# Preparing w_in's low parts: GpSimd adds up the high word's rest, and TensorE gathers three bfloat16 products

## The chip, the cores and the metric

The kernel runs on one core of a Trainium2 chip. The metric is the device time of one execution in microseconds. Several runs were timed; their median is quoted with the lowest and the highest.

## The reference

Eight sequences of 576 tokens go through block attention (8 heads of 64, blocks of 64 tokens that attend only within themselves) and then through a gated MLP with spatial gating. q and k come in scaled up, and the weights arrive as float64.

```python
scores = scale * np.matmul(q_c, k_c.transpose(0, 1, 2, 4, 3))
attn = np.exp(scores - np.max(scores, axis=-1, keepdims=True))
attn = attn / (np.sum(attn, axis=-1, keepdims=True) + 1e-09)
x = np.matmul(attn, v_c)              # then heads side by side: (8, 576, 512)

h = gelu_tanh(x @ w_in)               # w_in: 512 x 1024
u, v = h[..., :512], h[..., 512:]
v_n = (v - mean(v)) / np.sqrt(var(v) + 1e-06) * g_ln
v_s = np.einsum('ts,bsd->btd', w_sg, v_n) + b_sg[None, :, None]
out = x + (u * v_s) @ w_out           # w_out: 512 x 512
```

## The kernel before

**Precision.** Each operand of the MLP's products is kept as two fp32r numbers, a high part `hi` and a low part `lo`, and a product is the sum of three: lo x hi, hi x lo, hi x hi. The large weights come as float64, that is as two 32-bit words, and have to be turned into `hi` and `lo` on the chip. For w_in that is the work of `pair_begin` and `pair_end`, done eight times on pieces of 128 x 512 numbers: four pieces of the v half (one for each 128 rows, steps `W` and `w` of the start-up list) and four of the u half (one for each 128 columns, steps `X` and `x`).

**One piece.** It lands in a staging tile `st` of four words a number (the buffers that later hold w_sg or w_out's parts). `pair_begin` lets ScalarE (ACT) and VectorE (DVE) make three things from the two words: `f`, the high word's value as a float32; `p`, the power of two that belongs to it; and `q`, a bfloat16 that holds the upper bits of the low word on the scale of `p`. `pair_end` has ACT write `hi = -f`, rounded to fp32r. Then TensorE adds up in PSUM what is left: the identity in float32 times `f`, 2^-20 times `q`, -2^-20 times `p` (both in bfloat16, by the tiles `low`), and the identity in fp32r times `hi`. ACT negates the sum into `lo`. All weights of w_in carry a minus sign, which the activation behind the product takes off. In the v half, `v_w_end` then issues the load of a piece of the u half into the same staging tile.

**Order.** Steps of the first two sequences stand in a hand-written list, `START`: `L`, `W`, `w` load, begin and end a v piece, `X` and `x` begin and end a u piece, `S`, `T`, `O` (and `P`, `Q` for two tiles at a time) are scores, transposes and outputs of attention on tiles of 128 tokens, `G` and `g` load and split w_sg, `Y` prepares w_out, `A` loads q, k and v ahead, `D` keeps the TensorE clock up with spare products, and `vBM`, `uBM`, `sBM`, `oBM` are the four kinds of matmul units of the MLP for sequence B. In that phase attention, weight preparation and the first units are woven into each other on all engines. From sequence 2 on a loop runs v, u, s and o units with attention steps in fixed slots. The scheduler keeps each engine's instructions in an order of its own that follows the list, and each engine works through its order strictly one after another.

**Buffers.** The pool `ps_m` has three PSUM buffers `pm` of two banks each, handed out in turn to the scores of the first tiles, to the pieces' sums, and to the units. A unit's buffer comes free when ACT (`v`, `u`) or DVE (`s`, `o`) has read it.

**GpSimd (POOL)** does little: the low parts `xl` of two early tiles, the reciprocal root of the variance in `v_unit` (L461, a [128, 1] operation), and from the third sequence on the last multiplication of the softmax.

Lines that recur below: L130 to L133 `high_word`; L162 and L166 the rest of `pair_begin`; L174 `hi`; L178 the four products; L179 `lo`; L314 scores and L398 outputs of early tiles; L452 `v_unit`'s products, L455 its activation, L460, L461 and L467 to L470 its normalisation; L489 `u_unit`'s products; L509 `s_unit`'s.

Of the kernel before, what the change touches and what calls it, by code (L numbers as in the profile page):

```python
# [10 lines left out]
F32 = mybir.dt.float32  # L11
# [4 lines left out]
BF16 = mybir.dt.bfloat16  # L16
AF = mybir.ActivationFunctionType
ALU = mybir.AluOpType
# [4 lines left out]
P = 128  # L23
DM = 512
DF = 1024
DH = DF // 2
# [17 lines left out]

START = """
L0 A0 L1 A1 L2 L3 A4 W0 S0 W1 D8 w0 S1 W2 T0 w1 S2 O0 T1 W3 w2 S3 O1 T2 M0 w3 S4 O2 T3 v00 X0 O3 G0 T4 v01 x0 X1 O4 A8
v02 x1 X2 v03 X3 v04 u00 x2 g0 g1 u01 x3 g2 P5 g3 u02 g4 T5 u03 T6 s00 P7 Q5 s01 s02 T7 T8 s03 v10 Q7 v11 Y0 v12 Y1
v13 Y2 u10 Y3 u11 Y4 u12 Y5 Y6 u13 Y7 A10 s10 A12 s11 P9 s12 s13 T9 o00 T10 P11 o01 o02 o03 Q9 A14 T11 o10 T12 o11 Q11
S13 A15 o12 T13 o13
"""  # L50
# [30 lines left out]
def block_attention_gated_mlp(ctx: ExitStack, tc: tile.TileContext, qkv, w_in, w_out, w_sg, g_ln, b_sg, out):  # L81
    nc = tc.nc
# [7 lines left out]
    ps_m = ctx.enter_context(tc.tile_pool(name="ps_m", bufs=3, space=PSUM))  # L90
# [11 lines left out]
    ident_r = const.tile([P, P], F32R, name="ident")  # L102
    nc.scalar.copy(ident_r, eye)
    ident = ident_r.bitcast(F32)

    low = [const.tile([P, P], BF16, name=f"low_{i}") for i in range(2)]
    for a, c in zip(low, (2.0**-20, -(2.0**-20))):
        nc.scalar.mul(a, eye, c)
    win_h = const.tile([P, KT, DF], F32R, name="win_h")
    win_l = const.tile([P, KT, DF], F32R, name="win_l")  # L110
# [43 lines left out]
    def pair_begin(n, st):  # L154

        pair = st[:, : 2 * n].rearrange("p (n w) -> p n w", w=2)
        f, p = st[:, 2 * n : 3 * n], st[:, 3 * n : 4 * n]  # L160
        high_word(f, pair[:, :, 1])
        nc.vector.tensor_scalar(p, f, -0x800000, None, op0=ALU.bitwise_and)  # L162

        words = st[:, : 2 * n].bitcast(U16)
        q, lw, top = words[:, :n], words[:, 1::4], p.bitcast(U16)[:, 1::2]
        nc.vector.scalar_tensor_tensor(q, lw, 9, top, op0=ALU.logical_shift_right, op1=ALU.bitwise_or)  # L166

    def pair_end(n, hi, lo, st):

        f = st[:, 2 * n : 3 * n].bitcast(F32)  # L170
        p, q = st[:, 3 * n : 4 * n].bitcast(BF16)[:, 1::2], st[:, : 2 * n].bitcast(BF16)[:, :n]
        ps = ps_m.tile([P, 2, 512], F32, name="pm")[:, 0, :n]
        shape = lambda a: a.rearrange("p (k c) -> p k c", k=hi.shape[1]) if len(hi.shape) == 3 else a
        nc.scalar.mul(hi, shape(f), -1.0)  # L174
        terms = [(ident, f), (low[0], q), (low[1], p), (ident_r, hi)]
        for i, (a, c) in enumerate(terms):
            out_ps = shape(ps) if c is hi else ps
            nc.tensor.matmul(out_ps, a, c, start=(i == 0), stop=(i == len(terms) - 1))  # L178
        nc.scalar.mul(lo, shape(ps), -1.0)  # L179


    def w_out_tile(i, dt=F32R):
# [5 lines left out]
    staged = {}  # L188
# [3 lines left out]
        pair_begin(DH, staged["v", kt])  # L192

    def v_w_end(kt):
        pair_end(DH, win_h[:, kt, DH:], win_l[:, kt, DH:], staged["v", kt])
        u_w_load(kt)

    def v_w_load(kt):
# [3 lines left out]
    def u_w_load(dt):  # L202

        st = staged["u", dt] = w_sg_tile(dt, I32) if dt < 2 else w_out_tile(dt - 2, I32)
        dst = st[:, : 2 * DH].rearrange("p (k c) -> p k c", k=KT)
        nc.sync.dma_start(out=dst, in_=w_in[:, :, 2 * dt * P : 2 * (dt + 1) * P])

    def u_w_begin(dt):
        pair_begin(DH, staged["u", dt])

    def u_w_end(dt):
        cols = slice(dt * P, (dt + 1) * P)
        pair_end(DH, win_h[:, :, cols], win_l[:, :, cols], staged["u", dt])

    def o_w(et, half):
        nonlocal wout_h, wout_l
# [41 lines left out]
    def load_misc():  # L258
        nc.sync.dma_start(out=g_bc, in_=g_ln.broadcast_to([P, DH]))
# [44 lines left out]
    def att_scores(*tiles):  # L304

        scs = []
        for i, t in enumerate(tiles):
            qt = state[t]
            if t < PE_TILES:
                sc = ps_m.tile([P, 2, H, D], F32, name="pm")[:, 0]  # L310
                for h in range(H):
                    for c in range(2):
                        r = slice(c * D, (c + 1) * D)
                        nc.tensor.matmul(sc[r, h, :], qt[r, 0, h, :], qt[r, 1, h, :], start=True, stop=True)  # L314
            else:


                sc = banks[:, :, i * HP * D : (i + 1) * HP * D].rearrange("p c (hp s) -> p c hp s", hp=HP)
                for h in range(H):
                    for c in range(2):  # L320
                        r, o = slice(c * D, (c + 1) * D), slice((h + c) % 2 * D, ((h + c) % 2 + 1) * D)
                        nc.tensor.matmul(sc[o, c, h // 2, :], qt[r, 0, h, :], qt[r, 1, h, :], start=True, stop=True)  # L322
            scs.append(sc)
        for t, sc in zip(tiles, scs):
            softmax_begin(t, sc)
        for t in tiles:
            softmax_end(t)
# [57 lines left out]
    def att_out(*tiles):  # L385

        xos = []
        pm = ps_m.tile([P, 2, 512], F32, name="pm") if tiles[0] >= PE_TILES else None
        for i, t in enumerate(tiles):
            qt, ptT = state.pop(t)  # L390
            if t < PE_TILES:
                vt = qt[:, 2, :, :].rearrange("p (c hp) d -> p c hp d", c=2)
                xo = next_bank()
                for hp in range(HP):
                    for c in range(2):
                        for j in range(2):
                            r = slice(j * D, (j + 1) * D)
                            nc.tensor.matmul(  # L398
                                xo[r, hp, c * D : (c + 1) * D], vt[r, c, hp, :], ptT[r, hp, c * D : (c + 1) * D],
                                start=True, stop=True,  # L400
                            )
                xo = xo.rearrange("p hp (c s) -> p c hp s", c=2)
            else:

                xo = pm[:, :, i * HP * D : (i + 1) * HP * D].rearrange("p c (hp s) -> p c hp s", hp=HP)
                for h in range(H):
                    for c in range(2):
                        j, place = (h + c) % 2, c * HP + h // 2
                        r, o = slice(j * D, (j + 1) * D), slice(h % 2 * D, (h % 2 + 1) * D)
                        nc.tensor.matmul(  # L410
                            xo[o, c, h // 2, :], qt[r, 2, place, :], ptT[r, place].rearrange("p a s -> p (a s)"),
                            start=True, stop=True,
                        )
            xos.append(xo)
        for t, xo in zip(tiles, xos):
            keep(t, xo)
# [138 lines left out]
    def att_slots(b, n):  # L555
# [8 lines left out]
        return slots  # L564

    steps = {
        "L": v_w_load, "M": lambda k: load_misc(), "W": v_w_begin, "w": v_w_end, "X": u_w_begin, "x": u_w_end, "A": ahead,
        "S": att_scores, "T": att_transpose, "O": att_out, "P": lambda t: att_scores(t, t + 1), "Q": lambda t: att_out(t, t + 1),
    }
    for name, f in zip("vuso", (v_unit, u_unit, s_unit, o_unit)):  # L570
# [66 lines left out]
```

## Time and profile before

| | before |
|---|---|
| median of 3 runs | 507.87 us (507.09 to 510.36) |
| span of the profiled execution, first to last instruction | 505.7 us |
| PE busy | 493.4 us |
| DVE busy | 339.2 us |
| ACT busy | 274.2 us |
| POOL busy | 70.0 us |
| mean granted TensorE clock | 0.999 |

For the profiled execution the page gives its span; the runs' times stand beside it and take in launch and end. PE is TensorE's matmuls and PEld its weight loads. A row of the timeline has the start in microseconds from the span's start, the duration, the engine, the line, the operation, the output and inputs by the program's names, the shapes, and in brackets how long the engine had been idle and what ended that. "x2" joins two instructions of the same kind: the duration then runs from the first one's start to the last one's end. A matmul's duration includes the time in which its result drains, so that successive matmuls overlap in these rows. A row of the line view has the busy time and the mean of one in nanoseconds, or the shortest, the median and the longest.

### The profile page before, as it was taken

The numbers are of one execution on the slowest core, as the hardware profiler recorded it, in microseconds if no ns is written. First come the engines' busy times: TensorE is split into PE (matmuls) and PEld (weight loads), VectorE is DVE, ScalarE is ACT, GpSimd is POOL, SyncE is SP. The second block draws the span as 40 slices with busy tenths as digits, with TensorE's granted clock in tenths as the row PEclk, the third lists the DMA queues.
The fourth block names the chain that finished last, engine by engine and source line by source line (L and its number), as shares of the span: only waits on it lengthen the run. The fifth ranks groups of instructions, "written<-read, shape, count | busy, mean of one in ns | idle before, by whom it ended". The sixth has DMA issues, their size and how long they took to land.

```text
span 505.7 us, 12377 instructions
## 1 busy us (share of the span) xinstructions
PE 493.4 (98%) x5238; PEld 457.1 (90%) x5244; DVE 339.2 (67%) x707; ACT 274.2 (54%) x509; POOL 70.0 (14%) x72
## 2 busy tenths in 40 slices
PE   5999999999999999999999999999999999999996
PEld 4667899799998899989999899989999899999996
DVE  7998779987856947585563966676565776536141
ACT  5898667843346674355552774355643766334210
POOL 0112100210201401022100311022100131002000
PEclk9999999999999999999999999999999999999999
DMA  8958010237166113341324204160415200010002
GB/s 336 331 144 224 3 43 2 85 97 197 48 201 199 55 36 93 101 119 46 82 73 148 64 1 128 47 174 2 126 37 160 87 1 3 23 73 0 1 1 93
DMA packets 49595, 46.58 MB, mean 92 GB/s; under 512 B 35202, under 2 KB 39554, under 8 KB 49540
## 3 DMA queue, kind: packets, MB, share of 16 engines
q1 hardware_dynamic: 49540, 45.80, 29.9%
q8 instruction: 41, 0.67, 0.6%
q14 instruction: 14, 0.11, 0.1%
HBM read 36.34 MB, written 9.44 MB: 91 GB/s over the span
## 4 chain that ended last, share of the span: by engine, by line
PE 83%; DVE 7%; ACT 5%; DMA 3%; POOL 1%; issue 1%; DVEq 0%; SPq 0%; ACTq 0%; POOLq 0%
PE pm L509 20%; PE pm L532 19%; PE pm L489 18%; PE pm L452 17%; PE banks L322 3%; PE pm L410 3%; DMA qkv_t<-qkv 2%; PE pm L178 2%; DMA st<-w_out 1%; ACT pt L344 1%; PE pm L314 1%; POOL sm L461 1%; DVE v L470 1%; DVE gl L97 1%; PE pm L577 1%
## 5 line engine op out<-in xcount | busy, mean ns | idle before, releaser
L509 PE MATMUL pm<-wsg,v 128*128 128x288 f32 x768 | 107.9, 296 | 0.0
L509 PEld LDWEIGHTS pm<-wsg,v 128*128 128x128 f32 x768 | 103.9, 189 | 0.3
L532 PE MATMUL pm<-gh,wout 128*128 128x288 f32 x512 | 92.3, 297 | 0.0
L532 PEld LDWEIGHTS pm<-gh,wout 128*128 128x128 f32 x512 | 76.1, 189 | 0.5
L461 POOL TENSOR_TENSOR sm<-sm,neg_half 128x1 f32<-128x1 f32 x36 | 36.6, 1017 | 164.9 <-DVE sm L460 161.5
L358 POOL TENSOR_TENSOR pt<-pt,den 128x512 f32<-128x512 f32 x27 | 29.7, 1113 | 202.2 <-DVE den L357 128.3
L94 ACT CAST gh<-gt 128x576 fp32r<-128x576 f32 x32 | 21.5, 673 | 63.5 <-DVE gt L513 63.5
L532 PE MATMUL pm<-gl,wout 128*128 128x288 f32 x256 | 55.4, 296 | 0.0
L489 PE MATMUL pm<-xh,win_l 128*128 128x288 f32 x256 | 55.4, 298 | 0.0
L489 PE MATMUL pm<-xh,win_h 128*128 128x288 f32 x256 | 55.0, 296 | 0.0
L489 PE MATMUL pm<-xl,win_h 128*128 128x288 f32 x256 | 55.0, 296 | 0.0
L452 PE MATMUL pm<-win_h,xl 128*128 128x512 f32 x128 | 51.6, 403 | 2.0 <-DVE sm L460 0.9
L452 PE MATMUL pm<-win_l,xh 128*128 128x512 f32 x128 | 50.8, 397 | 0.0
L452 PE MATMUL pm<-win_h,xh 128*128 128x512 f32 x128 | 50.7, 396 | 0.0
L513 DVE TENSOR_TENSOR gt<-pm,u 128x576 f32<-128x576 f32 x32 | 24.1, 754 | 39.2 <-PE pm L509 39.1
L540 DVE TENSOR_TENSOR ot<-pm,xf 128x576 f32<-128x576 f32 (+1 forms) x33 | 24.1, 732 | 29.9 <-PE pm L532 29.8
L489 PEld LDWEIGHTS pm<-xh,win_l 128*128 128x128 f32 x256 | 41.5, 188 | 1.0
L532 PEld LDWEIGHTS pm<-gl,wout 128*128 128x128 f32 x256 | 41.5, 189 | 0.0
L489 PEld LDWEIGHTS pm<-xh,win_h 128*128 128x128 f32 x256 | 41.0, 188 | 0.0
L489 PEld LDWEIGHTS pm<-xl,win_h 128*128 128x128 f32 x256 | 41.0, 189 | 0.0
L97 DVE TENSOR_TENSOR xl<-pm,xh 128x512 fp32r<-128x512 f32 (+1 forms) x34 | 21.8, 640 | 26.4 <-ACT xh L94 26.4
L458 DVE BATCH_NORM_STATS2 sm<-hs 128x6 f32<-128x512 f32 x36 | 24.8, 688 | 19.8 <-ACT hs L455 19.6
(121 smaller groups left out, 816.7 us busy)
## 6 DMA issues: line engine op xcount, KB each, us to landing
qkv_t<-qkv SPq DMA_DIRECT2D x32, 512.0 KB, 4.5
out_dram<-ot SPq DMA_DIRECT2D x31, 288.0 KB, 2.1
qkv_t<-qkv SPq DMA_DIRECT2D x124, 64.0 KB, 3.6
qkv_t<-qkv SPq DMA_DIRECT2D x3, 768.0 KB, 11.9
wsg<-w_in SPq DMA_DIRECT2D x4, 512.0 KB, 6.4
wout<-w_in SPq DMA_DIRECT2D x4, 512.0 KB, 6.0
st<-w_out SPq DMA_DIRECT2D x8, 256.0 KB, 3.1
stage<-w_sg SPq DMA_DIRECT2D x5, 288.0 KB, 3.7
```

What stands on the lines that cost most here:

```text
L94: nc.scalar.copy(hi, src)
L97: lo_eng.tensor_tensor(lo, src, hi.bitcast(F32), op=ALU.subtract)
L322: nc.tensor.matmul(sc[o, c, h // 2, :], qt[r, 0, h, :], qt[r, 1, h, :], start=True, stop=True)
L358: (nc.gpsimd if t > last[1] else pick(f"n{t}")).tensor_tensor(pt, pt, den.unsqueeze(2).broadcast_to([P, H, D]), op=ALU.mult)
L452: nc.tensor.matmul(pv, a[:, kt, tok], c[:, kt, DH:], start=(i == 0), stop=(i == 11))
L458: nc.vector.bn_stats(st, h)
L461: nc.gpsimd.tensor_tensor(rs, rs, neg_half, op=ALU.pow)
L489: nc.tensor.matmul(pm[:, j, :HS], a[:, kt, dc], c[:, kt, j * HS : (j + 1) * HS], start=(i == 0), stop=(i == 11))
L509: nc.tensor.matmul(pm[:, j, :HS], a[:, dc], c[:, m, j * HS : (j + 1) * HS], start=(i == 0), stop=(i == len(ops) - 1))
L513: nc.vector.tensor_tensor(gt.rearrange("p (a c) -> p a c", a=2), pm[:, :, :HS], u2[0][:, dt, :].rearrange("p (a c) -> p a c", a=2), op=ALU ...
L532: nc.tensor.matmul(pm[:, j, :HS], a[:, kt, ec], c[:, kt, j * HS : (j + 1) * HS], start=(i == 0), stop=(i == len(ops) - 1),)
L540: nc.vector.tensor_tensor(ot[:, js], pm[:, js, :HS], res[:, js], op=ALU.add)
```

## The change

`pair_end` is cut in two. `pair_high` has ACT write `hi = -f` as before and then GpSimd compute `d = f + hi`, the part of `f` that `hi` does not hold, as a bfloat16, into the staging tile's second quarter of 16-bit words. The new `pair_end` adds up three bfloat16 products: `low[0]` times `q`, `low[1]` times `p`, and a bfloat16 identity times `d`. That identity, `ident_b`, is the upper half of each float32 of the old one. The float32 product with `f` and the fp32r product with `hi` go. For the v half both run in the step `w`, one behind the other. For the u half `x` now runs `pair_high` alone, and a new step `e` runs `pair_end`; in the list the `e` steps stand one or more units behind their `x`.

```diff
-v02 x1 X2 v03 X3 v04 u00 x2 g0 g1 u01 x3 g2 P5 g3 u02 g4 T5 u03 ...
+v02 e0 x1 X2 v03 e1 X3 v04 x2 u00 e2 x3 g0 g1 u01 e3 g2 P5 g3 u02 g4 T5 u03 ...
...
+    ident_b = ident_r.bitcast(BF16)[:, 1::2]
...
-    def pair_end(n, hi, lo, st):
-        f = st[:, 2 * n : 3 * n].bitcast(F32)
-        p, q = st[:, 3 * n : 4 * n].bitcast(BF16)[:, 1::2], st[:, : 2 * n].bitcast(BF16)[:, :n]
-        ps = ps_m.tile([P, 2, 512], F32, name="pm")[:, 0, :n]
+    def pair_parts(n, st):
+        words = st[:, : 2 * n].bitcast(BF16)
+        return words[:, :n], st[:, 3 * n : 4 * n].bitcast(BF16)[:, 1::2], words[:, n : 2 * n]
+
+    def pair_high(n, hi, st):
+        f, d = st[:, 2 * n : 3 * n].bitcast(F32), pair_parts(n, st)[2]
         shape = lambda a: a.rearrange("p (k c) -> p k c", k=hi.shape[1]) if len(hi.shape) == 3 else a
         nc.scalar.mul(hi, shape(f), -1.0)
-        terms = [(ident, f), (low[0], q), (low[1], p), (ident_r, hi)]
-        for i, (a, c) in enumerate(terms):
-            out_ps = shape(ps) if c is hi else ps
-            nc.tensor.matmul(out_ps, a, c, start=(i == 0), stop=(i == len(terms) - 1))
-        nc.scalar.mul(lo, shape(ps), -1.0)
+        nc.gpsimd.tensor_tensor(shape(d), shape(f), hi.bitcast(F32), op=ALU.add)
+
+    def pair_end(n, lo, st):
+        ps = ps_m.tile([P, 2, 512], F32, name="pm")[:, 0, :n]
+        for i, (a, c) in enumerate(zip((*low, ident_b), pair_parts(n, st))):
+            nc.tensor.matmul(ps, a, c, start=(i == 0), stop=(i == 2))
+        nc.scalar.mul(lo, ps.rearrange("p (k c) -> p k c", k=lo.shape[1]) if len(lo.shape) == 3 else ps, -1.0)
...
     def v_w_end(kt):
-        pair_end(DH, win_h[:, kt, DH:], win_l[:, kt, DH:], staged["v", kt])
+        pair_high(DH, win_h[:, kt, DH:], staged["v", kt])
+        pair_end(DH, win_l[:, kt, DH:], staged["v", kt])
         u_w_load(kt)
...
+    def u_w_high(dt):
+        pair_high(DH, win_h[:, :, dt * P : (dt + 1) * P], staged["u", dt])
     def u_w_end(dt):
-        cols = slice(dt * P, (dt + 1) * P)
-        pair_end(DH, win_h[:, :, cols], win_l[:, :, cols], staged["u", dt])
+        pair_end(DH, win_l[:, :, dt * P : (dt + 1) * P], staged["u", dt])
...
-        "X": u_w_begin, "x": u_w_end, ...
+        "X": u_w_begin, "x": u_w_high, "e": u_w_end, ...
```

More of the change, by code (lines that the diff above doesn't have):

```diff
@@ L46 @@
 L0 A0 L1 A1 L2 L3 A4 W0 S0 W1 D8 w0 S1 W2 T0 w1 S2 O0 T1 W3 w2 S3 O1 T2 M0 w3 S4 O2 T3 v00 X0 O3 G0 T4 v01 x0 X1 O4 A8
-v02 x1 X2 v03 X3 v04 u00 x2 g0 g1 u01 x3 g2 P5 g3 u02 g4 T5 u03 T6 s00 P7 Q5 s01 s02 T7 T8 s03 v10 Q7 v11 Y0 v12 Y1
+v02 e0 x1 X2 v03 e1 X3 v04 x2 u00 e2 x3 g0 g1 u01 e3 g2 P5 g3 u02 g4 T5 u03 T6 s00 P7 Q5 s01 s02 T7 T8 s03 v10 Q7 v11 Y0 v12 Y1
 v13 Y2 u10 Y3 u11 Y4 u12 Y5 Y6 u13 Y7 A10 s10 A12 s11 P9 s12 s13 T9 o00 T10 P11 o01 o02 o03 Q9 A14 T11 o10 T12 o11 Q11
@@ L566, in block_attention_gated_mlp @@
     steps = {
-        "L": v_w_load, "M": lambda k: load_misc(), "W": v_w_begin, "w": v_w_end, "X": u_w_begin, "x": u_w_end, "A": ahead,
+        "L": v_w_load, "M": lambda k: load_misc(), "W": v_w_begin, "w": v_w_end, "X": u_w_begin, "x": u_w_high, "e": u_w_end, "A": ahead,
         "S": att_scores, "T": att_transpose, "O": att_out, "P": lambda t: att_scores(t, t + 1), "Q": lambda t: att_out(t, t + 1),
```

## The prediction

> **What bounds the kernel now.** First the page's head, to see which engine could set the time:
>
> ```profile
> span 505.7 us, 12377 instructions
> PE 493.4 (98%) x5238; PEld 457.1 (90%) x5244; DVE 339.2 (67%) x707; ACT 274.2 (54%) x509; POOL 70.0 (14%) x72
> ```
>
> TensorE (PE) is busy in all but 12.3 us, GpSimd (POOL) in 70. That reads as "less PE work is less time". But the change touches only the preparation of w_in, all of it in the first 60 us, so I ask next what that stretch waits for. Here is the busy time of each engine in two stretches, cut where the chain of waits (below) returns to PE and where it leaves it again:
>
> ```profile
> core 0: us, PE busy (x) PEld busy (x) DVE busy (x) ACT busy (x) POOL busy (x), PEclk, DMA share, GB/s
> 10.00:37.70 27.70, 26.07 (x322) 17.76 (x324) 25.89 (x55) 25.10 (x78) 3.54 (x3) 1.00 0.76 254
> 37.70:70.70 33.00, 32.94 (x281) 27.92 (x287) 26.71 (x60) 25.81 (x46) 5.67 (x5) 1.00 0.34 89
> ```
>
> In 10 to 37.7 us three engines are nearly full: PE 26.1, VectorE (DVE) 25.9, ScalarE (ACT) 25.1 of 27.7 us. In 37.7 to 70.7 PE has 0.06 us to spare and DVE 6.3. The clock was 1.00 in both, so no duration here is stretched by it. Now the chain that ended last:
>
> ```profile
> 17.33 0.59 ACT xf L428
> ...
> 20.85 2.38 ACT pt L344 x16
> ...
> 25.03 1.10 DVE den L356
> ...
> 27.62 2.48 ACT pt L344 x16
> ...
> 37.07 0.65 DVE xl L97
> 37.76 1.43 PE pm L452 x5
> ...
> 66.92 3.73 PE pm L509 x28
> 70.67 0.77 DVE gt L513
> ```
>
> It is on PE up to 17.3 us (`xf` there waits for a PE product), alternates between ACT and DVE until DVE's `xl` frees `v02` at 37.76, is PE without a break to 70.67, and goes on from there through what that product starts. So a PE saving counts fully only between 37.76 and 70.67; before that, DVE and ACT have to be done with the same list of work as now. What starts at 70.67 hangs on PE's product, so I let a shift at that point pass to the end unchanged.
>
> **The change, part by part.** *PE's saving.* One pair's slot, x1's, from before:
>
> ```profile
> 42.48 1.02 PE L178 MATMUL pm<-wsg,ident 128*128 128x512 f32 x2
> 43.33 0.38 PE L178 MATMUL pm<-wsg,low 128*128 128x512 bf16 x1
> 43.58 0.59 PE L178 MATMUL pm<-win_h,ident 128*128 128x512 f32 x1
> 44.01 0.39 PE L452 MATMUL pm<-win_h,xl 128*128 128x512 f32 x1
> 44.24 0.40 PE L452 MATMUL pm<-win_l,xh 128*128 128x512 f32 x1
> 14.40 0.60 PE L178 MATMUL pm<-wsg,low 128*128 128x512 bf16 x2
> ```
>
> The float32 product is two instructions. PE is free for the next pair-unrelated product at 44.01, so the pair holds it for 44.01 - 42.48 = 1.53 us. The last row (two bfloat16 products in 0.60, one being 0.38) gives 0.22 us for each bfloat16 product; successive fp32r ones stand 44.24 - 44.01 = 0.23 apart. After: 3 x 0.22 = 0.66, a saving of 0.87 us a pair, 7.0 us for eight. The new stationary operand `ident_b` is every second bfloat16 of a float32 tile, and no row shows such a weight load. The nearest rows:
>
> ```profile
> L178 PEld LDWEIGHTS <-low x16: 97/98/98, 10.8 to 58.4; 128*128 128x128 bf16 x16
> L178 PEld LDWEIGHTS pm<-wsg,ident x8: 187/190/192, 10.2 to 42.5; 128*128 128x128 f32 x8
> ```
>
> Either, 0.10 or 0.19, fits beneath the 0.22 of the product running before it, so I take nothing (at most 0.1 x 8 = 0.8 if it were exposed).
>
> Where do the eight lie? Before, x1, x2 and x3 lie behind 37.76 (3 x 1.53 = 4.59). After, the list places x0's products (e0) behind `v02` too, so four lie there: 4 x 0.66 = 2.64. PE's stretch from 37.76 to 70.67 shrinks by **1.95 us**. That x0's 1.53 us vanish ahead of 37.76 brings nothing of itself: `v02` waits there for DVE's `xl`, not for PE.
>
> *ACT and VectorE.* Their instructions stay: same negation into `hi`, same eviction into `lo`, same bit operations. Nothing gets shorter on the two engines that carry the chain from 17.3 to 37.7.
>
> *GpSimd's eight sums.* `d = f + hi`, 128x512 float32 with two full inputs. The nearest row is GpSimd's `xl` subtraction; beside it what DVE did meanwhile, and the same DVE operations undisturbed:
>
> ```profile
> 18.65 1.28 POOL L97 TENSOR_TENSOR xl<-xf,xh 128x512 fp32r<-128x512 f32 x1 [17.35 <-ACT xh L94]
> 19.18 1.30 DVE L133 SCALAR_TENSOR_TENSOR wout<-wout 128x512 int32<-128x512 int32 x1
> 15.37 0.68 DVE L133 SCALAR_TENSOR_TENSOR wout<-wout 128x512 int32<-128x512 int32 x1
> 24.82 1.27 POOL L97 TENSOR_TENSOR xl<-xf,xh 128x512 fp32r<-128x512 f32 x1 [4.89 <-ACT xh L94]
> 25.03 1.09 DVE L356 TENSOR_SCALAR den<-den 128x8 f32<-128x8 f32 x1
> 30.21 0.17 DVE L356 TENSOR_SCALAR den<-den 128x8 f32<-128x8 f32 x1
> L358 POOL TENSOR_TENSOR pt<-pt,den 128x512 f32<-128x512 f32 x27 | 29.7, 1113 | 202.2 <-DVE den L357 128.3
> ```
>
> A sum should take 1.28 us (between 1.11, the mean with a broadcast input, and, if the bfloat16 output costs more, 2.2, the longest two-input operation GpSimd has here, shown below). More telling is the DVE column: beside GpSimd the L133 took 1.30 instead of 0.68, and an L356 of 0.17 took 1.09 and ended at 26.12, just after GpSimd at 26.09. DVE was held until GpSimd was done: 0.62 and 0.92 us lost, mean 0.77. The first started 0.53 us into GpSimd's 1.28: until then DVE ran a reduction out of PSUM, which was not held.
>
> The Trainium skill ("SBUF — State Buffer", section "SBUF: two separate sides") gives the reason: the two engines share a port pair under "an exclusive lock, not a bandwidth split", taken by GpSimd or by a DVE operation with two SBUF inputs or in a two-port mode, whichever is first, for its whole length. The trace agrees (1.09 against 0.17). By that rule alone a sum that meets only such operations would cost DVE its full 1.28, 10.2 us for eight; the rows above, where part of each sum ran beside a PSUM reader, are what I use.
>
> Most of DVE's list around the sums is of the held kinds (L131 to L133, L162, L166, L356, L358). Ahead of 37.76 lie five sums (w0 to w3, x0): 5 x 0.77 = **3.85 us** of DVE. What can swallow it: DVE's idle time in 10 to 37.7, which is 27.7 - 25.89 = 1.81, of which these waits for others are genuine slack:
>
> ```profile
> 13.16 0.69 DVE L333 TENSOR_REDUCE nmax<-pm 128x8 f32<-128x512 f32 x1 [0.28 <-PE pm L314]
> 23.26 0.17 DVE L356 TENSOR_SCALAR den<-den 128x8 f32<-128x8 f32 x1 [0.27 <-ACT pt L344]
> 32.52 0.70 DVE L458 BATCH_NORM_STATS2 sm<-hs 128x6 f32<-128x512 f32 x1 [0.62 <-ACT hs L455]
> 17.33 0.58 ACT L428 COPY xf<-banks 128x512 f32<-128x512 f32 x1 [0.61 <-PE banks L398]
> ```
>
> 0.28 + 0.27 + 0.62 = 1.17, and from the last row 0.3 of the 0.61 us in which ACT waits for PE, since w0 and w1 are 0.87 shorter each but the next ACT step, w2's `hi`, hangs on DVE. Carried to 37.76: 3.85 - 1.17 - 0.3 = **+2.4 us** (bounds: 0 if the sums meet PSUM readers and idle time, 5 x 1.28 - 0.3 = 6.1 if they meet nothing else). After 37.76 DVE has 6.3 us of slack and three sums cost it 2.3: I take nothing.
>
> *The new wait.* PE's third product waits for ACT `hi`, then GpSimd's 1.28; before, the last product waited for `hi` alone, with 1.3 us of other products ahead of it. Behind it on PE's queue stand scores and transposes. The latest `hi` of the v pairs is w3's:
>
> ```profile
> 24.58 0.69 ACT L174 ACTIVATE win_h<-wout 128x512 fp32r<-128x512 f32 x1
> 55.57 0.75 DVE L256 TENSOR_TENSOR wsg<-bt,bh 1x576 fp32r<-1x576 f32 x1
> ```
>
> It ends at 25.27, GpSimd's `xl` above at 26.09, so `d` is there at about 27.4. `v00` reads the fourth low part in its last three products of twelve, and `v01` waits for DVE anyway, so I take nothing (0 to 1). w3's buffer is released about 2 us later, so on SP's queue the u load behind it, and the qkv and w_sg loads behind that, start as much later; the page gives that load 6.0 us to land, from about 28, and ACT begins x3 some 9 us after that start: hidden. The splits of w_sg must wait for e0 and e1, which read the buffers they go to, some 4 us; DVE's last instruction for them, the second row, ended at 56.3, and `s00` needs them 10 us later: hidden.
>
> **Sum:** -1.95 + 2.4 = about **+0.4 us** on the profiled 505.7, so 506.1. The median of the runs shown, 507.87, is 2.2 above that span (launch and end); predicted 508.3, no change. A measurement of this kernel can tell about 1%, 5.1 us, from none.
>
> **The rivals.** (1) *The holding does not reach PE*: the sums fall into stretches where DVE reads PSUM or waits, and the order of each engine adapts. Then the PE saving stands alone: 505.7 - 1.95 = 503.8 on the span, and with up to 1.2 us of DVE's early waits gone 502.6; plus 2.2, and in the middle of the two, **505.4**. For it: POOL's idle time gives much freedom; against: both rows with GpSimd beside DVE in this stretch show a loss.
>
> (2) *GpSimd's queue becomes the wait* (the slower side). v_unit's reciprocal root (L461) is on the same in-order queue:
>
> ```profile
> 33.70 0.99 POOL L461 TENSOR_TENSOR sm<-sm,neg_half 128x1 f32<-128x1 f32 x1 [7.61 <-DVE sm L460]
> 45.69 2.19 POOL L461 TENSOR_TENSOR sm<-sm,neg_half 128x1 f32<-128x1 f32 x1 [0.97 <-DVE sm L460]
> 47.92 0.72 ACT L469 ACTIVATE v<-hs,sm 128x512 fp32r<-128x512 f32 x1 [1.06 <-POOL sm L461]
> 48.55 0.58 ACT L455 ACTIVATE hs<-pm 128x512 f32<-128x512 f32 x1
> 32.85 0.64 ACT L174 ACTIVATE win_h<-wsg 128x512 fp32r<-128x512 f32 x1
> 49.60 0.43 PE L489 MATMUL pm<-xh,win_l 128*128 128x288 f32 x2
> ```
>
> x0's `hi` (32.85 + 0.64) is ready just before the root at 33.70, and x3's comes about when the one at 45.69 starts. If a sum stands ahead of the root, L469 comes 1.28 later, and behind it in ACT's order the eviction of `v03` (L455, 48.55 to 49.13). The three PSUM buffers then decide: with e1 and e2 at their new places, `u00` (PE, 49.60) takes the buffer that `v03` gives back, a margin of 0.47 us. Two such delays, at x0 and x3, cost 2 x 1.28 = 2.6 on top of my sum: **510.9**. It decides as soon as a sum runs within 0.5 us ahead of a root.
>
> (3) *All of the saving counts*, since early PE time draws the DVE and ACT work forward: -7.0 gives **500.9**. Against it: they have only 1.8 and 2.6 us idle in 27.7.
>
> (4) *It doesn't do what it says*: sums of 2.2 us, as in the second row above, hold DVE 2.19 - 1.28 = 0.9 longer, five times ahead of 37.76: 508.3 + 4.5 = **512.8**.
>
> **How the numbers follow.** Forecast (506.5 to 510) 0.45; rival 1, 0.25; rival 2, 0.18; rival 3, 0.05; rival 4, 0.07. Leaving out rivals 3 and 4 and a little of the edges, the range is 503.9 to 512.0. Faster by over 1% is below 502.8: rival 3 and a tail of rival 1, 0.08. Slower by over 1% is above 512.9: half of rival 4 and the tail of rival 2, 0.09. Within: 0.83.
>
> **What would show it.** In the changed profile: L178-like rows with three bfloat16 products at 0.38 each and no float32 ones; eight new GpSimd rows of about 1.3 us; DVE's busy time up by 4 to 6 us with an unchanged count, in L131 to L166 and L356 rows that read 1.0 to 1.3; `v02` starting near 40 instead of 37.76; PE idle in 10 to 40 us up by some 6 us; `s00` starting within 1 us of 66.75. I am wrong if DVE's rows stay at their old lengths, if `v02` starts before 37 or after 42, or if ACT's waits for L461 grow by over 2 us.

## The result, and the profile after

The changed kernel takes **511.72 us** in the median (511.11 to 512.65, 4 runs), against 507.89 us for the kernel before on the same chip: ratio 1.0075, 95% interval 1.005 to 1.01. It is 3.8 us slower. That lies within the bound of 1% and, by 0.3 us, within the predicted range (up to 512.0), but 3.4 us above the predicted 508.3 and nearer to rival 2 (510.9). The profiled execution has a span of 510.0 us, 4.3 more than before. In the experiments below, three plainly disturbed executions (686, 1667 and 2680 us) are part of the medians but not of the ratios.

Lines have moved: the products are L185 now, `hi` L177, the sum L179, `lo` L186, `v_unit`'s products L462, its root L471, the activation behind the root L479, softmax L368. From the page of the changed kernel, the head:

```profile
span 510.0 us, 12371 instructions
PE 490.7 (96%) x5228; PEld 456.9 (90%) x5228; DVE 342.2 (67%) x707; ACT 274.3 (54%) x509; POOL 82.4 (16%) x80
```

TensorE has 2.7 us less to do and the span is 4.3 us longer. So the time is in waits. VectorE has the same 707 instructions and 3.0 us more. The same stretches as in the prediction, cut where `v02` and the product behind `s00` now stand (us, busy time of each engine with its instructions, granted clock, DMA share, GB/s):

```profile
10.00:41.40 31.40, 23.84 (x316) 17.65 (x315) 28.47 (x56) 24.38 (x76) 10.79 (x9) 0.89 0.68 228
41.40:75.25 33.85, 32.59 (x276) 27.77 (x280) 27.20 (x57) 26.60 (x47) 10.14 (x8) 0.95 0.32 83
```

`v02` starts at 41.40 instead of 37.76, 3.64 later. Up to there DVE has 28.47 us of work instead of 25.89, with one instruction more. From there to the end of `s00`'s first products it is 33.85 us instead of 32.9. And the clock is no longer 1.00 in either stretch. What DVE waited for, ahead of `v02`:

```profile
DVE nmax L343 <- PE pm L324: 2.0, 2, 1.7
```

Before, that wait was 0.28. So the 3.64 consist of 2.58 us of longer DVE work and 1.06 of longer DVE idle time, the latter because scores come late from PE (1.7 more) while DVE's wait for `hs` (0.62) is gone. The rest is best seen at two places of the timeline, both in this fence, with a line of dots between them:

```profile
18.28 1.26 POOL L97 TENSOR_TENSOR xl<-xf,xh 128x512 fp32r<-128x512 f32 x1 [3.40 <-ACT xh L94]
18.40 1.69 DVE L167 SCALAR_TENSOR_TENSOR wout<-wout 128x512 uint16<-128x512 uint16 x1
20.14 0.93 PE L185 MATMUL pm<-wout,low 128*128 128x512 bf16 x2 [2.83 <-DVE wout L167]
...
39.33 0.15 DVE L470 TENSOR_SCALAR sm<-sm 128x1 f32<-128x1 f32 x1
39.44 1.83 POOL L179 TENSOR_TENSOR wsg<-wsg,win_h 128x512 bf16<-128x512 f32 x1 [3.96 <-ACT wout L131]
40.67 0.67 DVE L97 TENSOR_TENSOR xl<-banks,xh 128x512 fp32r<-128x512 f32 x1
41.23 0.55 POOL L471 TENSOR_TENSOR sm<-sm,neg_half 128x1 f32<-128x1 f32 x1
41.40 0.50 PE L462 MATMUL pm<-win_h,xl 128*128 128x512 f32 x1 [2.13 <-DVE xl L97]
41.81 0.72 ACT L479 ACTIVATE v<-hs,sm 128x512 fp32r<-128x512 f32 x1 [1.92 <-POOL sm L471]
43.61 0.65 PE L376 MATMUL banks<-ident,pt 128*128 128x128 f32 x4 [1.26 <-ACT xf L442]
```

At 18.40 GpSimd's `xl`, an old instruction, holds DVE's making of `q`, which takes 1.69 instead of 0.69. PE, whose first product of that piece reads `q`, stands for 2.83 us. Before, the float32 product of `f` stood first in the piece and did not need `q`; the change removed it, and with it PE's cover. The second place is the lower part: x1's sum takes GpSimd until 41.27, the root behind it on the queue had its input from DVE since 39.48, ACT's L479 stands 1.92 us for that root, and then PE 1.26 for ACT's `xf` behind it. Now the clock around those places, PE alone, in steps of 3.4 us cut where the clock changes:

```profile
core 0: us, PE busy (x), PEclk, DMA share, GB/s
16.88:20.30 3.42, 0.59 (x17) 1.00 0.95 311
20.30:23.71 3.41, 3.02 (x17) 0.50 0.03 8
23.71:27.12 3.41, 3.41 (x59) 0.50 0.72 238
40.78:44.19 3.41, 1.53 (x8) 1.00 0.85 260
44.20:47.60 3.40, 3.40 (x37) 0.50 0.86 265
```

Behind the first stall PE is nearly full and runs at half speed for 6.8 us, behind the second for 3.4 us. That makes three candidates: the holding of DVE by the sums, the queue of GpSimd, and PE's stalls with the clock that falls behind them.

### The profile page after: what moved, and what is told of

The parts are those of the page before. It is cut to its first block, busy times and chain, and to the rows that moved or that the text cites. A ratio compares the mean times of both kernels' runs of the same rounds, so it can differ in the third digit from the quotient of the medians.

```text
span 510.0 us, 12371 instructions
## 1 busy us (share of the span) xinstructions
PE 490.7 (96%) x5228; PEld 456.9 (90%) x5228; DVE 342.2 (67%) x707; ACT 274.3 (54%) x509; POOL 82.4 (16%) x80
## 4 chain that ended last, share of the span: by engine, by line
PE 87%; DVE 8%; ACT 2%; issue 1%; DMA 1%; POOL 0%; DVEq 0%; SPq 0%; ACTq 0%
PE pm L519 21%; PE pm L499 20%; PE pm L542 19%; PE pm L462 18%; PE banks L332 3%; PE pm L420 3%; PE pm L324 1%; DMA qkv_t<-qkv 1%; PE pm L185 1%; DVE nmax L343 1%; PE banks L408 1%; DVE gl L97 1%; DVE gt L523 1%; DVE pt L368 1%; DVE blocks L382 1%
## 5 line engine op out<-in xcount | busy, mean ns | idle before, releaser
L368 POOL TENSOR_TENSOR pt<-pt,den 128x512 f32<-128x512 f32 x27 | 29.7, 1113 | 202.0 <-DVE den L367 128.0
L471 POOL TENSOR_TENSOR sm<-sm,neg_half 128x1 f32<-128x1 f32 x36 | 37.1, 1031 | 151.9 <-DVE sm L470 148.3
L462 PE MATMUL pm<-win_h,xl 128*128 128x512 f32 x128 | 52.2, 408 | 3.5 <-DVE xl L97 2.6
L462 PE MATMUL pm<-win_l,xh 128*128 128x512 f32 x128 | 51.0, 399 | 0.0
L462 PE MATMUL pm<-win_h,xh 128*128 128x512 f32 x128 | 50.8, 397 | 0.0
## 6 DMA issues: line engine op xcount, KB each, us to landing
qkv_t<-qkv SPq DMA_DIRECT2D x32, 512.0 KB, 4.6
wsg<-w_in SPq DMA_DIRECT2D x4, 512.0 KB, 6.1
wout<-w_in SPq DMA_DIRECT2D x4, 512.0 KB, 6.2
```

What stands on the lines that cost most here:

```text
L368: (nc.gpsimd if t > last[1] else pick(f"n{t}")).tensor_tensor(pt, pt, den.unsqueeze(2).broadcast_to([P, H, D]), op=ALU.mult)
L462: nc.tensor.matmul(pv, a[:, kt, tok], c[:, kt, DH:], start=(i == 0), stop=(i == 11))
L471: nc.gpsimd.tensor_tensor(rs, rs, neg_half, op=ALU.pow)
```

## The experiments

In the expectations, theory A lays the loss on held DVE, on the stalls of PE that follow, and on the clock behind them; theory B lays it on GpSimd's sums holding DVE, without the clock; theory C on the missing float32 products alone. Times and ratios are against the kernel before on the same chip (507.65 us for the first four runs, 508.0 for the next four, 507.92 for the last three).

**Only the sums.** The old four products, and beside them the eight sums, whose result nobody reads:

```diff
         nc.scalar.mul(hi, shape(f), -1.0)
+        nc.gpsimd.tensor_tensor(shape(st[:, : 2 * n].bitcast(BF16)[:, n : 2 * n]), shape(f), hi.bitcast(F32), op=ALU.add)
         terms = [(ident, f), (low[0], q), (low[1], p), (ident_r, hi)]
```

> The kernel before, with its four products a piece, and GpSimd's eight sums added beside them; nobody reads the sums, so this is their cost by itself. Three theories of the 3.8 us that the change lost. A: DVE is held by the sums, PE then waits longer, and where it waits over 2 us its clock falls to half, so both the sums and the missing products have a part. B: the holding of DVE alone. C: the missing float32 products alone, which had covered waits of PE and kept its clock up. A expects 1 to 3 us over the kernel before, with the clock at 1.00 throughout. B expects 4 to 6 us over (the loss of 3.8 and the 2 that the products save). C expects no difference within 1 us.

512.43 us, ratio 1.009 (1.0067 to 1.0112), +4.8 us. No instruction reads these sums and PE has all its old products, and still it is as slow as the whole change. A's and C's numbers are missed, B's is hit. `v02` starts at 43.04. DVE's total rises by 6.7 us, to 345.9, and a row of its timeline shows how, beside a sum from 9.12 to 10.51:

```profile
8.96 0.42 DVE L131 TENSOR_SCALAR wsg<-wsg 128x512 f32<-128x512 f32 x1
9.42 1.38 DVE L132 TENSOR_SCALAR wsg<-wsg 128x512 int32<-128x512 int32 x1
13.07 1.60 DVE L359 TENSOR_TENSOR pt<-pt,den 128x512 f32<-128x512 f32 x1
```

L132 takes 0.42 alone and 1.38 here; L359, 0.69 alone, takes 1.60 beside the sum at 12.85. In the profiled execution the clock fell once (0.94 in 10 to 41 us), behind a PE wait of 2.02 us for that L359. The other three executions had a clock of 1.000 and took 512.31 to 513.21 us, so this loss needs no fall of the clock. GpSimd's queue has a part here: x0's sum keeps `v00`'s root waiting for 1.77 us. But that root's input from DVE was 3.8 us late already (37.40 instead of 33.61), with no root queued before it, and both `xl` operations ahead of it found GpSimd idle.

**Only the products.** The change without the sums; the third product reads `p` again, so the kernel leaves the rest of the high word out of the low part:

```diff
-        nc.gpsimd.tensor_tensor(shape(d), shape(f), hi.bitcast(F32), op=ALU.add)
-        for i, (a, c) in enumerate(zip((*low, ident_b), pair_parts(n, st))):
+        for i, (a, c) in enumerate(zip((*low, ident_b), (*pair_parts(n, st)[:2], pair_parts(n, st)[1]))):
```

> The changed kernel without the sums: the third bfloat16 product reads p in place of d, so the rest of the high word is left out of the low part; PE's load and order are those of the change, GpSimd has nothing new. A expects between 3 us under the kernel before and no gain, with some PE gaps ahead of 38 us and perhaps one fall of the clock. B expects 2 to 4 us under it. C expects 2 to 4 us over it, with the clock at half for about as long as in the changed kernel (some 11 us).

506.86 us, 0.9977 (0.9967 to 0.9988), -0.8 us. A's number is hit; B's 2 to 4 us under and C's 2 to 4 over are missed. So B has the cost of the sums right and the worth of the saved products wrong. 4.8 and -0.8 add up to +4.0, and the change gives +3.8, so the two parts nearly add up. PE's 5.6 us less in total (487.8 against 493.4) are worth 0.8.

**Half of the pieces.** The changed kernel with the old `pair_end`, under the name `pair_end_old`, for the v half, so that only the u half is new:

```diff
     def v_w_end(kt):
-        pair_high(DH, win_h[:, kt, DH:], staged["v", kt])
-        pair_end(DH, win_l[:, kt, DH:], staged["v", kt])
+        pair_end_old(DH, win_h[:, kt, DH:], win_l[:, kt, DH:], staged["v", kt])
```

And with the old one, and the old list, for the u half:

```diff
     def u_w_high(dt):
-        pair_high(DH, win_h[:, :, dt * P : (dt + 1) * P], staged["u", dt])
+        cols = slice(dt * P, (dt + 1) * P)
+        pair_end_old(DH, win_h[:, :, cols], win_l[:, :, cols], staged["u", dt])
```

> The change made for the four u pieces alone; the v pieces keep the float32 and fp32r products and have no sum. PE's order up to the third unit is that of before. A expects the saving of the stretch in which PE is the limit to come through: 2 us under the kernel before (1 to 3), clock 1.00. B expects about 1 us over, since four of eight sums stay and cost half of 4 to 6 against a saving of 2. C expects 2 us under as A does.

> The change made for the four v pieces alone, with the list of before; the u pieces keep their products and have no sum. A expects 3 to 5 us over the kernel before, the wait of PE for w2's q of over 2 us and the clock at half behind it. B expects 2 to 3 us over, with no need for a fall of the clock. C expects 3 to 5 us over, whatever DVE's rows show.

u alone: 509.01 us, 1.0029 (1.0015 to 1.0043). v alone: 510.70, 1.0051 (1.0032 to 1.007). Both are slower, and together they make +4.4 against the change's +3.8. For the u half A and C expected a gain of 2, which is missed; B's 1 over is close. For the v half 3.05 is at the edge of all three. The profiled execution of the u half is the fastest of ten (508.39); its clock stayed at 0.999, so its 0.7 us are not the clock's. Seven executions with 0.997 took 508.5 to 509.3, and two with 0.993 took 510.9: part of the median's 1.36 goes with the clock. In the fastest a single hold on the path to `v02` can be seen in the timeline, DVE and GpSimd of the u-only kernel:

```profile
33.98 1.88 DVE L488 SCALAR_TENSOR_TENSOR hs<-hs,sm,g_bc 128x512 f32<-128x512 f32 x1
...
34.01 1.30 POOL L179 TENSOR_TENSOR wsg<-wsg,win_h 128x512 bf16<-128x512 f32 x1 [7.48 <-ACT win_h L177]
35.27 1.00 POOL L482 TENSOR_TENSOR sm<-sm,neg_half 128x1 f32<-128x1 f32 x1
```

x0's sum takes GpSimd just ahead of `v00`'s root, which comes 1.2 late, and DVE's normalisation takes 1.88 instead of 0.74. In the v-only kernel it is otherwise: its last sum and its first root on GpSimd are

```profile
24.52 1.27 POOL L179 TENSOR_TENSOR wout<-wout,win_h 128x512 bf16<-128x512 f32 x1 [2.72 <-ACT win_h L177]
38.90 0.99 POOL L484 TENSOR_TENSOR sm<-sm,neg_half 128x1 f32<-128x1 f32 x1 [8.76 <-DVE sm L483]
```

No root stands behind a sum, and PE waits for GpSimd's sums for 0.8 us in all. So its 3.05 us are not the queue of the roots; its DVE total is 2.7 us longer. Its clock lay at 0.992 to 0.997 in the four executions, and the one at 0.997 was no faster (510.95).

**The clock, filled.** Spare products put into the two gaps of the changed kernel:

```diff
-... O0 T1 W3 w2 S3 O1 ...
+... O0 T1 W3 D6 w2 S3 O1 ...
...
-v02 e0 x1 X2 ...
+D6 v02 e0 x1 X2 ...
```

> The changed kernel with spare products (identity by identity, float32, 128 columns, read by nobody) in its two long PE gaps: six steps' worth ahead of w2's products and six around v02's start. They depend on nothing, so they fill waits that PE has anyway. If the clock's fall behind these gaps costs the changed kernel 2 to 4 us, as its half-speed rows from 20 to 27 and from 44 to 47.6 us suggest, the clock stays at 1.00 and the time comes down to 508 to 510. If the fall is harmless, because PE is not the limit where it is slow, the time stays within 0.7 us of 511.7.

510.78 us, 1.0054 (1.0036 to 1.0072), about 1 us better than the change, though the intervals overlap. In the profiled execution the first fall is gone, the second one stayed:

```profile
10.00:41.40 31.40, 24.93 (x339) 1.00 0.69 234
41.40:48.00 6.60, 6.51 (x50) 0.74 0.99 265
```

Yet `v02` starts at 41.48, as in the change (41.40): with full clock up to there nothing was won, since DVE has 28.3 us of work in these 31.4 (28.5 in the change) and now waits 2.1 us for ACT instead of 2.0 for PE. The expected 508 to 510 is missed, and 510.78 lies just under the other range, 511.0 to 512.4. So the stall and the fall at 18 to 28 us do not set when `v02` starts; they are a consequence, not the main cause. The second fall was not filled in the profiled execution, but one execution of this kernel had a clock of 0.999, with hardly any fall, and took 510.56 us: 2.6 us of loss are left without the clock.

**The sum on DVE.** For all eight pieces, and for the u half alone:

```diff
-        nc.gpsimd.tensor_tensor(shape(d), shape(f), hi.bitcast(F32), op=ALU.add)
+        nc.vector.tensor_tensor(shape(d), shape(f), hi.bitcast(F32), op=ALU.add)
```

> The changed kernel with the eight sums on DVE in place of GpSimd. A two-input operation of 128x512 takes DVE 0.69 us, so DVE's list grows by 5.5 us; nothing holds it, and the 1.3 us of waiting for GpSimd go. If a sum on GpSimd costs DVE about as much as DVE's own sum would (the kernel with idle sums had DVE busy 6.7 us longer, 0.84 a sum), the time is at most that of the change, 509.5 to 511.7. If GpSimd really took work off DVE, it is over 513.

> The change made for the four u pieces alone, with their sums on DVE. With the sums on GpSimd this was 509.0 against 507.65. In the stretch from v02 to s00 PE is the limit and DVE has some 6 us to spare, four sums of 0.69 are 2.8. If the holding by GpSimd and the place of its sums ahead of the roots ate the saving, 505.5 to 507. If it is the added DVE work or the order of the list that costs, 508 to 510.

510.82 us, 1.005 (1.0031 to 1.0069), and 509.26, 1.0031 (1.0013 to 1.0049): beside 1.0075 and 1.0029 with GpSimd, and both intervals overlap those. The first is as expected; the second hits the branch that puts the cost on the added DVE work or the list. But with the sums on DVE the time goes with the clock from one execution to the next: with eight, 508.5 to 509.2 us at 0.995 and 512.1 to 512.3 at 0.987; with the u half, 507.23 at 0.998 and 511.5 to 511.6 at 0.993. From the line view of the first, whose profiled execution is its fastest:

```profile
L179 DVE TENSOR_TENSOR wsg<-wsg,win_h x4: 658/684/691, 9.0 to 36.4; 128x512 bf16<-128x512 f32 x4
```

On DVE a sum costs 0.68 us, and DVE's total rises by 3.5 us with eight of them. On GpSimd it takes 1.27 or more and lengthens DVE by 0.4 to 1.0 us (3.0, 2.7, 4.0 and 6.7 us over eight, four, four and eight sums, in the change, v alone, u alone and the sums alone). So with eight sums GpSimd relieved DVE of little or nothing.

**The list.** `e` directly behind its `x`, as the old list had it:

```diff
-... v01 x0 X1 O4 A8 v02 e0 x1 X2 v03 e1 X3 v04 x2 u00 e2 x3 g0 g1 u01 e3 g2 ...
+... v01 x0 e0 X1 O4 A8 v02 x1 e1 X2 v03 X3 v04 u00 x2 e2 g0 g1 u01 x3 e3 g2 ...
```

> The changed kernel with e directly behind x in the list, that is the u pieces' products where they stood before. If the new places of e in the list (and with them the turn of the three PSUM buffers) cost time, it is faster than the change by 1 us or more. If they help by hiding GpSimd's 1.3 us, it is slower by 0.5 to 2 us. If the loss is DVE being held, the list matters little: within 0.7 us of 511.7.

510.94 us, 1.0056 (1.0038 to 1.0074), `v02` at 41.33. It is 0.8 us under the change, between the two ranges expected (over 1, within 0.7), and the intervals overlap. The position of `e` decides little.

**GpSimd busy, but not reading.** In place of each sum three zero fills of `d`:

```diff
-        nc.gpsimd.tensor_tensor(shape(d), shape(f), hi.bitcast(F32), op=ALU.add)
+        for _ in range(3):
+            nc.gpsimd.memset(d, 0.0)
```

> The changed kernel with GpSimd's sum replaced by three fills of d with zero, one behind the other: the rest of the high word is left out of the low part, PE still waits for GpSimd and GpSimd's queue is as long, but GpSimd reads nothing. If DVE being held by the sums is what costs, the time falls to 507 to 508.5, close to the kernel without sums (506.9), and DVE's two-input rows keep their 0.69 us beside the fills. If the wait for GpSimd and its queue cost, it stays at 510.5 to 512.

507.71 us, 1.0001 (0.9991 to 1.0012), as expected if the holding is what costs: 4.0 us of the change's time are gone, while GpSimd's queue is as full as before (POOL 84.2 us against 82.4), PE's products wait for its result, and the clock still falls (0.94 in 10 to 38 us). The same piece as in the row of the sums alone:

```profile
9.18 2.08 POOL L180 MEMSET wsg<- 128x512 bf16 x3 [7.87 <-DVE nmax L351]
9.51 0.71 DVE L133 TENSOR_SCALAR wsg<-wsg 128x512 int32<-128x512 int32 x1
10.25 0.69 DVE L134 SCALAR_TENSOR_TENSOR wsg<-wsg 128x512 int32<-128x512 int32 x1
```

DVE's two-input L134 is not held at all, its one-input row a little (0.71 for 0.42), and DVE's total is 339.6 us, that of before within 0.4. The fills do not wait for `hi`, and a root stands behind a single fill at most (0.37 and 0.63 us late, against 1.75 in the change), so this run takes away most of those waits too. The other runs tell them apart. With the sums alone PE waits for no sum; in the v-only kernel no root stands behind one; they lost 4.8 and 3.05 us. What both have and the fills lack is GpSimd reading beside DVE, so the reading is the main cause. Against the run without sums (-0.8 us) the fills cost 0.6 by the medians and 1.2 by the ratios: that much is left for the queue and a wait for its result.

The Trainium skill ("SBUF — State Buffer", section "Who interferes with whom") says that a DVE instruction with two SBUF inputs contends with a GpSimd instruction that reads SBUF, and not with one that only writes it. The rows agree: 0.69 beside the fills, 1.60 beside a sum.

**Where DVE has time.** The new way for u's pieces 2 and 3 alone, which lie behind `v02`, with their `x` and `e` at the change's places; and the same with the sums on DVE. Against the change, beside the v half's old way as above:

```diff
-v02 e0 x1 X2 v03 e1 X3 v04 x2 u00 e2 x3 g0 g1 u01 e3 g2 ...
+v02 x1 X2 v03 X3 v04 x2 u00 e2 x3 g0 g1 u01 e3 g2 ...
...
+        if dt < 2:
+            pair_end_old(DH, win_h[:, :, cols], win_l[:, :, cols], staged["u", dt])
+        else:
+            pair_high(DH, win_h[:, :, cols], staged["u", dt])
```

> An attempt to beat both kernels: only the u pieces 2 and 3 get the new products, with sums on GpSimd; pieces 0 and 1 and the v pieces stay as before. Their sums come behind v02's start, where PE was the limit and DVE has its longest pauses (47.5 to 48.7 and from 58 us). Saving of PE 2 x 0.87 = 1.7; if the two sums fall into DVE's pauses, 506 to 507 against 507.9. If holding DVE eats it again, 507.5 to 509.

> The same two u pieces with their sums on DVE, 2 x 0.69 us there and no wait for GpSimd. If the saving of 1.7 us passes, 506 to 507, and it tells whether GpSimd or DVE is the better place for a sum in a stretch with slack; if the pieces' later ends delay the u units as in the run with four sums on DVE, 508 to 509.

With GpSimd: **506.07 us, 0.9963 (0.995 to 0.9976)**, 1.85 us faster than the kernel before, as expected, and faster than the change. From its chain of waits:

```profile
38.38 1.43 PE pm L477 x5
...
43.26 1.53 PE pm L198 x5
44.79 5.60 PE pm L477 x24
50.39 3.20 PE pm L514 x24
53.59 0.68 PE pm L185 x3
54.26 3.20 PE pm L514 x24
57.46 0.67 PE pm L185 x3
58.13 1.09 PE banks L347 x64
59.23 6.59 PE pm L514 x48
65.82 3.73 PE pm L534 x28
```

An old piece takes 1.53 on PE and a new one 0.67, the stretch is PE without a break, and from `v02` (38.38) to `s00` (65.65) it is 27.27 us instead of 29.0: 1.73 saved, two times 0.87. The holds are there, and harmless, since nothing on the chain waits for DVE here:

```profile
45.87 1.30 POOL L179 TENSOR_TENSOR wout<-wout,win_h 128x512 bf16<-128x512 f32 x1 [0.53 <-DVE wout L167]
45.99 1.47 DVE L163 TENSOR_SCALAR wout<-wout 128x512 int32<-128x512 int32 x1
48.91 1.70 POOL L179 TENSOR_TENSOR wout<-wout,win_h 128x512 bf16<-128x512 f32 x1 [0.33 <-DVE wout L167]
49.38 1.79 DVE L495 SCALAR_TENSOR_TENSOR v<-hs,sm,v 128x512 fp32r<-128x512 f32 x1
```

With the sums on DVE: 509.97 us, 1.0037 (1.0024 to 1.0049), 3.9 more, and over both expected ranges. From its waits and PE's stretches:

```profile
PE pm L514 <- ACT u L521: 2.4, 1, 2.4
62.00:64.00 2.00, 2.00 (x10) 0.53 0.00 0
64.00:66.00 2.00, 2.00 (x12) 0.61 0.04 8
```

One PE gap of 2.38 us, up to 61.81, and then half clock in most of 4 us (0.47 and 0.39 of 2 us lost, 1.7 in all): 4.1, about as much as `s00` comes later (69.82 against 65.65). The gap is a wait for ACT's `u`, and two roots on GpSimd took 2.1 and 2.3 us here against 0.99 with the sums on GpSimd. So for these two pieces, where DVE has slack, GpSimd was the better place, while with eight sums the two places did not differ clear of the noise. That the long roots made the gap is argued from the rows; why a root takes 2.2 us at some times is not settled.

## Why the prediction was right and wrong

*PE's saving.* Right in size: a new piece takes 0.67 us (0.66 predicted), the strided weights cost nothing, and where nothing else changes two pieces save 1.73 us. Right, too, that what is saved ahead of `v02` is worth nothing: all eight without sums gave 0.8 us, less even than the 1.95 forecast for the part behind `v02`.

*The sums, 1.28 us each.* The undisturbed ones take 1.27 to 1.29; with their own waits for DVE the median is 1.5, up to 1.83. Rival 4's 2.2 did not come.

*Each sum holds DVE, `v02` +2.4.* The mechanism is what the fills, the sums alone and the v half alone show. Six sums lie ahead of `v02`, not five, since x1's starts before it too. The size was off in three terms that partly cancel. The net hold in the change was 0.37 us a sum (3.0 over eight; "DVE busy up by 4 to 6" is missed) rather than 0.77; in the other runs it was 0.7 to 1.0. The 1.17 us of slack were not there to swallow it: DVE's idle time grew by 1.06. And that a held DVE stops PE, now that the float32 product no longer stands first, and that scores then come back late to DVE, has no term. The sum says 40.2, measured is 41.40, inside the given 37 to 42. That it comes so close is in part luck.

*After 37.76: "I take nothing", and "The new wait": "I take nothing".* This is the step that failed. The stretch from `v02` to the end of `s00`'s first products should have shrunk by 1.95 and grew by 0.94, 2.9 us worse. The trace has 1.26 us of PE standing for ACT behind the root, which stood behind x1's sum: rival 2's mechanism, with a delay of 1.75 us at one place where I priced 1.28 at two. The rest is the clock, at half speed for 3.4 us with PE full, so that 1.7 us of work wait. I had weighed that delay but given it 0.18, although its own condition, a sum within 0.5 us ahead of a root, was easy to meet with eight sums and five roots in 50 us. The sign given for it, ACT's waits for the root up by over 2 us, did not show: they went from 3.9 to 4.7 us between 10 and 76 us. That those 2.9 us split as the trace suggests is argued, not shown: no run put the sum behind the root.

*The clock.* "No duration here is stretched by it" held for before and was carried over without asking what a PE wait of 2 to 3 us does to it. The clock adds to the loss in places (above), but the sums alone lost 4.8 us with and without a fall.

*A shift at `s00` passes to the end.* Right: 4.6 us there, 4.3 in the span, 3.8 in the median. In u23 1.1, 1.4 and 1.85.

*The range.* 511.72 lies within it because the range was drawn wide enough for rival 2 (510.9), not because of the sum, which forecast no change.

*The rivals.* Rivals 1 and 3 fell with the first rows. Rival 1's condition, that the holding does not reach PE, is met in u's pieces 2 and 3, and there the saving does stand alone.

What stays open is the exact split of the 3.8 us between holding, queue and clock in the changed kernel: about 4 go with the reading, 0.6 to 1.2 stand for the queue and the wait for its result, and filling the first gap gave back about 1, within the noise; these overlap.

## What to carry to other kernels

Ask of each piece of saved work whether its engine ends a wait at that place: eight savings of 0.87 us gave 0.8 us, two of them at the right place 1.85. An elementwise operation given to GpSimd was hardly taken off VectorE here, since both read SBUF meanwhile; look at VectorE's rows beside the GpSimd rows already in the trace, and put it where VectorE has slack and no root or other short step stands behind it on GpSimd's queue. When products are removed, ask which wait they had covered on PE.

## What was not expected of the hardware

How little idle time halves PE's clock, and that the length of the gap does not decide it. The kernel without sums, then the u-only kernel:

```profile
18.43 0.38 PE L184 MATMUL pm<-wout,low 128*128 128x512 bf16 x1 [1.55 <-DVE wout L167]
21.00:22.00 1.00, 1.00 (x24) 0.50 0.94 284
```

```profile
39.32 0.50 PE L473 MATMUL pm<-win_h,xl 128*128 128x512 f32 x1 [2.96 <-DVE xl L97]
40.00:41.00 1.00, 1.00 (x8) 1.00 0.98 292
```

A gap of 1.55 us, with PE busy for 0.83 of the 3 us from 17 to 20, was followed by half speed; one of 2.96 with full work on both sides was not. In every trace in which the clock falls it changes at steps of 3.41 us (in the change at 20.30, 27.12, 44.2 and 47.6). With all traces cut into these steps from 10 us on, every step at full clock in which PE is busy for 1.53 us or less, ten in all, is followed by a step at half speed, and none with 1.85 or more is; between 1.6 and 1.8 both occur. The gap of 1.55 lies in a step with 1.48 us busy; the one of 2.96 is split between two with 2.15 and 1.71. The Trainium skill ("TensorE: Matmul & The Clock Gate", section "Part 1: The HAM clock gate (the "warmup" mystery)") tells of a free-running window of about 3.4 us that must be idle. The length of the window and its fixed position agree with these steps; that it must be wholly idle does not: here a step less than half busy was enough.
